# Sparse attention with a feed-forward block: keys fetched by DMA into place, values as whole rows by indexed DMA, transposes of P in two PSUM tiles

## The chip, the cores and the metric

The kernel runs on one core of one Trainium2 chip, as one launch. The metric is device time in microseconds (us). Before the change it is 954.41 us, the median of three runs (954.15 to 954.64). One further run was profiled: it took 950.94 us, and its trace spans 949.2 us from the first to the last instruction.

## The reference

Block-sparse attention feeds a layer norm and a two-layer feed-forward block (FFN) with a residual:

```python
# q, k, v: (4, 8, 768, 64) f32; sampled_blocks: (24, 3) int64, ids of key blocks of 32
scores = q @ k^T / 8
mask = |block_i - block_j| <= 1, or block_i or block_j in {0, 23},
       or block_j in sampled_blocks[block_i]
attn = softmax(where(mask, scores, -1e9)) @ v          # heads side by side: x (4, 768, 512)
xn = (x - mean) / sqrt(var + 1e-6) * g_ln
out = x + relu(xn @ w_ch1) @ w_ch2                      # w_ch1 512x2048, w_ch2 2048x512, float64
```

A query block of the middle attends eight key blocks: three sampled, block 0, its three neighbours and block 23. Query blocks 0 and 23 attend all 24. Sampled blocks are data: the program reads their ids at run time.

## The kernel before

**Tiles and visits.** Each of the 4 batches has 6 query tiles of 128 rows, in the order 1, 2, 3, 0, 4, 5. Tiles 1 to 5 (kind N) hold four middle blocks and are done in 2 visits of four heads. Tile 0 holds blocks 1, 2, 0, 23: it takes four visits of kind D (the two dense blocks, all 24 key blocks) and one of kind H (blocks 1 and 2). That is 15 visits a batch, 60 in all, counted from 0.

**A visit.** TensorE (PE) makes the scores in `ps` (L204), VectorE (DVE) the row maximum (L237, L240), ScalarE (ACT) the exponentials `p` (L247). PE transposes `p` into PSUM tile `pt` in two halves of four matmuls (L257), and ACT copies each half to SBUF (L258). One visit later PE multiplies by the values `vs` into `pv` (L267), and DVE divides by the row sum (L296 to L313). `ps` and `pt` are single PSUM tiles of two banks each.

**Keys.** All 24 key blocks of a batch lie in `kx`, loaded by plain DMA. For each N or H tile DVE copies the blocks of each query block from there into `ks` (L139 sampled, L140 neighbours, L146 blocks 0 and 23), with ids loaded into DVE registers (L122).

**Values.** Each visit of kind N or H loads its own rows of 1040 B (four heads) by DMAs that SyncE (SP) issues: one for the neighbours (L159), two or three for blocks 0 and 23 (L164), and twelve of 32 rows each whose block is a register (L179). They go into a ring of two tiles `vs`. Sampled ids that repeat a block of the mask are replaced by a block of zeros.

**FFN.** Float64 weights come as bit pairs, 1 MB pieces for w1 and 0.5 MB for w2, and are turned into an f16 high and low part by DVE (L401, L403, L405), ACT (L410, L411) and GpSimd (POOL, L412). Two w1 pieces are split in each of visits 0 to 3, four w2 pieces in each of visits 4 to 7. ACT issues the loads of all pieces but the first four. The FFN works on pairs of tiles (the first and the last tile alone): up matmuls into `pu` (L349), ACT and DVE evict (L359, L360), down matmuls into `pd` (L372).

**Order.** It is written out by a loop over steps; step s holds the scores of visit s, the value matmuls of visit s-1, and a share of the FFN's matmuls, spread over tasks such as the copies of keys, the splits and the transposes. Engines execute their instructions in that order.

Of the kernel before, what the change touches and what calls it, by code (L numbers as in the profile page):

```python
# [25 lines left out]
def sparse_attention_moe(  # L26
# [4 lines left out]
    v: bass.AP,  # L31
# [21 lines left out]
    ps_t = ctx.enter_context(tc.tile_pool(name="ps_t", bufs=1, space=bass.MemoryType.PSUM))  # L53
# [10 lines left out]
    kx = const.tile([P, NB, P], F32, name="kx")  # L64
    ks_s = ring("ks", 2, [P, 4, 8, P], F32)
# [24 lines left out]
    samp = const.tile([1, 2 * NB * NR], I32, name="samp")  # L90
    bid = const.tile([1, NB, 1], F32, name="bid")
    si = const.tile([1, NB, NR], I32, name="si")
    ei = const.tile([1, NB, NR], I32, name="ei")
    sf = const.tile([1, NB, NR], F32, name="sf")
    cf = const.tile([1, NB, NR], F32, name="cf")
    tf = const.tile([1, NB, NR], F32, name="tf")

    def index_a():
        nc.vector.tensor_copy(si, samp.rearrange("o (n r t) -> o n r t", r=NR, t=2)[:, :, :, 0])

    def index_b():
        nc.vector.tensor_copy(sf, si)
        nc.vector.tensor_tensor(out=cf, in0=sf, in1=bid.to_broadcast([1, NB, NR]),
# [14 lines left out]
        nc.vector.tensor_copy(ei, tf)  # L118

    def ids(table, eng, first, count, top):  # L120
        flat = table.rearrange("o n r -> o (n r)")[0:1, first * NR : (first + count) * NR]
        _, vals = nc.values_load_multi_w_load_instructions(  # L122
            flat, engines=[eng], min_val=0, max_val=top, skip_runtime_bounds_check_because=WHY)
        return vals

    def load_k(b, lo, hi, dma):
        dma.dma_start(kx[:, lo:hi, :], kT[b, :, lo:hi, :])

    def load_q(n, dma):
# [12 lines left out]
    def edges(t):  # L142
        ks = ks_s[t.n % 2]
        n = 2 if t.t == 0 else 4
        for s, e in ((3, 0), (7, NB - 1)):
            nc.vector.tensor_copy(ks[:, 0:n, s, :], kx[:, e : e + 1, :].to_broadcast([P, n, P]))  # L146

    def values(vi, dma):
        src, vs = v[vi.b], vi.vs
        if vi.kind == "D":  # L150
            if vi.fresh:
                dma.dma_start(vs[:, 0:6, :],
                              src[vi.hf, 0 : 6 * P, :].rearrange("(c p) e -> p c e", p=P))
            yield
            return
        if vi.kind == "N":
            i0 = vi.first
            s = src[vi.hf]
            dma.dma_start(vs[0:96, 1::2, :],  # L159
                          bass.AP(s.tensor, s.offset + (i0 - 1) * BLK * HV,  # L160
                                  [[HV, 96], [BLK * HV, 4], [1, HV]]))

            def spread(dst, blk, n):
                dma.dma_start(dst, bass.AP(s.tensor, s.offset + blk * BLK * HV,  # L164
                                           [[HV, BLK], [0, n], [1, HV]]))

            spread(vs[96:128, 0::2, :], 0, 4)
            if i0 + 3 < NB - 2:
                spread(vs[96:128, 1::2, :], NB - 1, 4)
            else:  # L170
                spread(vs[96:128, 1:7:2, :], NB - 1, 3)
                spread(vs[96:128, 7:8, :], NB, 1)
            for gg in range(4):
                if gg == 2:
                    yield
                if gg % 2 == 0:
                    reg = ids(ei, ET.SP, i0 + gg, 2, NB)
# [3 lines left out]
        else:  # L181
            sr = src.rearrange("f r e -> r f e")
            reg = ids(ei, ET.SP, 1, 2, NB)
            for gg in range(2):
                i = 1 + gg
                dma.dma_start(vs[0:96, 4 * gg + 2 : 4 * gg + 4, :],
                              sr[(i - 1) * BLK : (i + 2) * BLK])
                dma.dma_start(vs[96:128, 4 * gg + 2 : 4 * gg + 4, :],
                              sr[(NB - 1) * BLK : NB * BLK])
                e = NB if i == 1 else 0  # L190
                dma.dma_start(vs[96:128, 4 * gg : 4 * gg + 2, :], sr[e * BLK : (e + 1) * BLK])
                for r in range(NR):
                    dma.dma_start(vs[32 * r : 32 * r + 32, 4 * gg : 4 * gg + 2, :],
                                  sr[bass.ds(reg[3 * gg + r] * BLK, BLK)])
                if gg == 0:
                    yield
        yield

    def scores(vi):
        ps = vi.ps = ps_s.tile([P, 1024], F32, tag="ps", name=f"ps{vi.i}")  # L200
        q, ks = q_s[vi.tile.n % 2], ks_s[vi.tile.n % 2]
# [48 lines left out]
    def turn(vi):  # L250
        pt = ps_t.tile([P, 8, P], F32, tag="pt", name=f"pt{vi.i}")
        c = vi.shape[0] * vi.shape[1] // P
        dst = pt_s[vi.i % 2]
        for lo in range(0, c, 4):
            hi = min(c, lo + 4)
            for k in range(lo, hi):
                nc.tensor.transpose(pt[:, k, :], p_s[:, k * P : (k + 1) * P], id_sb)  # L257
            nc.scalar.copy(dst[:, lo:hi, :], pt[:, lo:hi, :])  # L258

    def attn_v(vi):  # L260
        pt, vs = pt_s[vi.i % 2], vi.vs
# [10 lines left out]
        if vi.kind == "N":  # L272
            for h in vi.heads:
                for c in range(2):
                    for gg in range(4):
                        mm(gg, h % 4, (2 * (h % 2) + h % 4 // 2) * 2 + c, 2 * gg + c, h % 4, c)
        elif vi.kind == "H":
            for pp in range(2):
                for j in range(2):
                    for c in range(2):  # L280
                        for rr in range(2):
                            h = 4 * pp + 2 * rr + j
                            for gg in range(2):
                                mm(2 * rr + gg, 2 * pp + j, (2 * j + pp) * 2 + c,
                                   4 * gg + 2 * c + h // 4, h % 4, c)
        else:
            for c in range(6):
                for rr in range(2):
                    for gg in range(2):
                        mm(2 * rr + gg, 0, c, c, 2 * rr + vi.r % 2, c)  # L290
# [44 lines left out]
    def ffn(u):  # L335
# [29 lines left out]
        for t in u.tiles:  # L365
# [3 lines left out]
            for f in range(FT):  # L369
                assert (2, f) in split  # L370
# [17 lines left out]
    con1 = stg  # L388
# [25 lines left out]
    def split_w1(i):  # L414
        fs = slice(i * 256, (i + 1) * 256)
        split_w(raw1[i % 4], con1[i % 2], w1h[:, :, fs], w1l[:, :, fs], SW1)
        split.add((1, i))
        if i + 4 < 8:
            load_w1(i + 4, nc.scalar)

    def split_w2(i):
        split_w(raw2[i % 4], con2[i % 2], w2h[:, i, :], w2l[:, i, :], SW2)
        split.add((2, i))
        if i + 4 < 16:
            load_w2(i + 4, nc.scalar)
# [14 lines left out]
    nv = 0  # L440
    for t in tiles:
        if t.t:
            plan = [("N", f, f, list(range(4 * f, 4 * f + 4))) for f in range(2)]
        else:
            plan = [("D", r // 2, r, [4 * (r // 2) + r % 2, 4 * (r // 2) + r % 2 + 2])
                    for r in range(4)] + [("H", 0, 0, list(range(8)))]
        t.visits = []
        for kind, hf, r, heads in plan:
            vi = SimpleNamespace(i=len(visits), kind=kind, hf=hf, r=r, b=t.b, tile=t,
                                 first=4 * t.t - 1, heads=heads,  # L450
                                 shape=(1, 768) if kind == "D" else (4, 256))
            vi.fresh = not (kind == "D" and r % 2)
            nv += vi.fresh
            vi.vs = vs_s[nv % 2]
            visits.append(vi)
            t.visits.append(vi)
# [8 lines left out]
    nc.sync.dma_start(samp, sampled.bitcast(I32))  # L465
    nc.scalar.dma_start(bid.rearrange("o n x -> o (n x)"), blocks)
    for lo in range(0, NB, 6):
        load_k(0, lo, lo + 6, (nc.sync, nc.scalar)[lo // 6 % 2])
    load_q(0, nc.sync)
    for i in range(4):  # L470
        load_w1(i, nc.gpsimd)
    nc.scalar.dma_start(id_sb, eye)
    nc.scalar.dma_start(g_sb, g.to_broadcast([P, DM]))
    nc.vector.memset(eps, 1e-6)
    index_a()
    index_b()
    for gg in range(4):
        keys(tiles[0], gg)
    edges(tiles[0])
    for i in range(8):  # L480
        at(i // 2, split_w1, i)
    for i in range(4):
        at(3, load_w2, i, nc.scalar)
    for i in range(16):
        at(4 + i // 4, split_w2, i)
    for t in tiles[1:]:
        prev = tiles[t.n - 1].visits
# [127 lines left out]
```

## Time and profile before

| | before |
|---|---|
| median of three runs | 954.41 us |
| profiled execution, and its span | 950.94 us, 949.2 us |
| PE busy | 737.7 us (78%) |
| DVE, ACT, POOL busy | 387.8, 283.4, 83.8 us |
| mean granted TensorE clock | 0.923 |
| DMA | 97.06 MB, mean 102 GB/s |

PE is the busiest engine. The page's slices show two regimes: in the first fifth PE is busy 1 to 5 tenths, then mostly 9, with dips to 6 to 8 that come back at even distances, once a batch.

### The profile page before, as it was taken

The page shows a single profiled execution, that of the slowest core. Times are in us where ns is not written, and L with a number is a line of the kernel's source. Part 1 is how long each engine was busy: PE and PEld are TensorE (multiplying, and loading weights), DVE is VectorE, ACT ScalarE, POOL GpSimd, SP SyncE. Part 2 cuts the span into 40 slices and gives each one's busy share as a digit, 9 for nine tenths or more (in the row PEclk, how much of TensorE's full clock was granted, in tenths as well). Part 3 has the DMA queues.
Part 4 walks back from the last instruction along what each step waited for, and adds up shares of the span by engine and source line. Part 5 has one row for each costly group of instructions (what it writes and reads, how often), then busy time and mean ns, then how long its engine had stood idle before and what let it go on. Part 6 is the DMA issues. An engine that isn't in the chain of part 4 may idle for free.

```text
span 949.2 us, 23159 instructions
## 1 busy us (share of the span) xinstructions
PE 737.7 (78%) x9344; PEld 486.4 (51%) x9344; DVE 387.8 (41%) x996; ACT 283.4 (30%) x553; POOL 83.8 (9%) x80
## 2 busy tenths in 40 slices
PE   1222455797789999996699899997699999977997
PEld 0111342473375574663375664753574755733855
DVE  5486477433434343342344252352352443342301
ACT  1243344242233232242133241332232422422201
POOL 1242223100000000000000000000000000000000
PEclk9955678899989999998799999997899999989999
DMA  8634744223643533224835432334634442234010
GB/s 302 184 117 121 215 135 133 70 59 84 158 114 61 131 78 102 57 64 101 182 73 101 108 98 73 75 66 137 129 79 110 114 113 57 58 87 95 2 32 15
DMA packets 98607, 97.06 MB, mean 102 GB/s; under 512 B 38083, under 2 KB 89412, under 8 KB 97476
## 3 DMA queue, kind: packets, MB, share of 16 engines
q1 hardware_dynamic: 92546, 71.39, 32.8%
q10 hardware_dynamic: 3458, 13.70, 4.3%
q0 software_dynamic: 2496, 10.49, 3.1%
q8 instruction: 74, 1.21, 0.6%
q14 instruction: 33, 0.27, 0.1%
HBM read 82.94 MB, written 6.29 MB: 94 GB/s over the span
## 4 chain that ended last, share of the span: by engine, by line
issue 67%; PE 8%; SPq 7%; DMA 5%; DVE 5%; POOL 4%; ACT 3%; DVEq 0%; ACTq 0%; POOLq 0%
DMA vs<-v 5%; PE pu L349 4%; SPq L179 3%; POOL xl L328 2%; SPq L122 2%; PE pt L257 1%; PE ps L204 1%; POOL out L380 1%; PE pd L372 1%; SPq L164 1%; DVE st L237 1%; ACT pt L258 1%; PE pv L267 1%; DVE ot L403 1%; ACT ot L410 1%
## 5 line engine op out<-in xcount | busy, mean ns | idle before, releaser
L257 PE MATMUL pt<-id_sb,p 128*128 128x128 f32 x448 | 78.2, 295 | 137.1 <-ACT pt L258 129.8
L349 PEld LDWEIGHTS <-w1h 128*128 128x128 f16 x1664 | 154.5, 100 | 19.3 <-issue 0.7
L247 ACT ACTIVATE p<-ps,st 128x256 f32<-128x256 f32 (+1 forms) x192 | 83.3, 510 | 262.9 <-DVE rs L296 167.8
L372 PE MATMUL pd<-w2h,hh 128*128 128x512 f16 x384 | 148.9, 388 | 0.0
L372 PE MATMUL pd<-w2h,hl 128*128 128x512 f16 x384 | 148.3, 386 | 0.0
L372 PE MATMUL pd<-w2l,hh 128*128 128x512 f16 x384 | 148.0, 385 | 0.0
L360 DVE SCALAR_TENSOR_TENSOR hl<-pu,hh 128x512 f16<-128x512 f32 x96 | 66.4, 691 | 195.1 <-ACT hh L359 195.0
L257 PEld LDWEIGHTS pt<-id_sb,p 128*128 128x128 f32 x448 | 51.8, 146 | 161.8 <-ACT pt L258 144.4
L349 PE MATMUL pu<-xth,w1h 128*128 128x256 f16 (+1 forms) x832 | 123.0, 270 | 0.0
L349 PE MATMUL pu<-xth,w1l 128*128 128x256 f16 (+1 forms) x832 | 122.5, 269 | 0.0
L372 PEld LDWEIGHTS <-hh 128*128 128x128 f16 x768 | 75.9, 99 | 89.1 <-issue 6.9
L349 PE MATMUL pu<-xtl,w1h 128*128 128x256 f16 (+1 forms) x832 | 120.9, 267 | 0.0
L267 PE MATMUL pv<-vs,pt 128*32 128x65 f32 x3584 | 79.0, 235 | 44.0 <-DMA vs<-v 43.9
L258 ACT COPY pt<-pt 128x512 f32<-128x512 f32 x120 | 67.0, 559 | 147.1 <-PE pt L257 136.1
L237 DVE TENSOR_REDUCE st<-ps 128x4 f32<-128x1024 f32 (+1 forms) x60 | 69.1, 1151 | 89.5 <-PE ps L204 89.1
L267 PEld LDWEIGHTS pv<-vs,pt 128*32 128x32 f32 x3584 | 64.3, 118 | 75.4 <-issue 59.8
L359 ACT ACTIVATE hh<-pu 128x512 f16<-128x512 f32 x96 | 57.5, 599 | 146.6 <-PE pu L349 146.6
L349 PEld LDWEIGHTS <-w1l 128*128 128x128 f16 x832 | 79.0, 100 | 9.0
L139 DVE COPY ks<-kx 128x128 f32 x264 | 56.3, 269 | 63.0 <-issue 42.5
L204 PE MATMUL ps<-ks,q 64*32 64x256 f32 x1408 | 53.3, 416 | 25.0 <-DVE ks L146 15.5
L378 DVE SCALAR_TENSOR_TENSOR ot<-pd,x 128x512 f32<-128x512 f32 x24 | 16.6, 691 | 133.8 <-PE pd L372 133.8
L328 POOL TENSOR_TENSOR xl<-xn,xh 128x512 f16<-128x512 f32 x24 | 27.6, 1151 | 458.8 <-ACT xh L327 452.8
(62 smaller groups left out, 432.2 us busy)
## 6 DMA issues: line engine op xcount, KB each, us to landing
vs<-v SPq DMA_DIRECT2D x488, 32.5 KB, 1.8
vs<-v SPq DMA_DIRECT2D x40, 390.0 KB, 4.3
vs<-v SPq DMA_DIRECT2D x72, 130.0 KB, 4.3
vs<-v SPq DMA_DIRECT2D x8, 780.0 KB, 4.6
q<-qT SPq DMA_DIRECT2D x24, 256.0 KB, 2.9
out<-ot POOLq DMA_DIRECT2D x24, 256.0 KB, 2.4
kx<-kT SPq DMA_DIRECT2D x6, 768.0 KB, 7.5
stg<-w ACTq DMA_DIRECT2D x8, 512.0 KB, 3.8
```

The source lines that it names most:

```text
L139: cp(ks[:, gg, r : r + 1, :], kx[:, bass.ds(t.reg[3 * (gg % 2) + r], 1), :])
L204: nc.tensor.matmul(ps[32 * part : 32 * part + 32, col : col + n], lhs[64 * row : 64 * row + 64], rhs[64 * row : 64 * row + 64], start=True ...
L237: nc.vector.tensor_reduce(out=st[:, 0:n], in_=vi.ps[:, 0 : n * w].rearrange("p (h k) -> p h k", k=w), axis=AX.X, op=ALU.max, negate=True)
L247: nc.scalar.activation(p_s[:, hs], vi.ps[:, hs], AF.Exp, bias=vi.st[:, 4 + h : 5 + h], scale=0.125)
L257: nc.tensor.transpose(pt[:, k, :], p_s[:, k * P : (k + 1) * P], id_sb)
L258: nc.scalar.copy(dst[:, lo:hi, :], pt[:, lo:hi, :])
L267: nc.tensor.matmul(pv[32 * row : 32 * row + 32, 65 * col : 65 * col + 65], pt[:, ch, 32 * row : 32 * row + 32], vs[:, vv, 65 * e : 65 * e ...
L328: nc.gpsimd.tensor_sub(xl, xn, xh)
L349: nc.tensor.matmul(ph[:, j * n : (j + 1) * n], w[:, ct, fs], x[:, ct, 0:n], start=m == 0, stop=m == 3 * CT - 1, skip_group_check=True)
L359: nc.scalar.activation(dh, ph, AF.Relu)
L360: nc.vector.scalar_tensor_tensor(out=dl, in0=ph, scalar=0.0, in1=dh, op0=ALU.max, op1=ALU.subtract)
L372: nc.tensor.matmul(po, x[:, f, ts], w[:, f, :], start=m == 0, stop=m == 3 * FT - 1)
```

## The change

- **Keys.** `kx` and the DVE copies are gone. `ks` is a ring of two tiles of 32 blocks. For an N or H tile SP issues one DMA for the neighbours (1536 B pieces) and 12 (H: 6) of one block each, 128 partitions of 512 B, with register ids. Blocks 0 and 23 stand in a small tile `kg` per batch and POOL copies them in (L168). For the dense blocks the 24 blocks are loaded into a ring tile in two DMAs.
- **Values.** One load per job (a tile; tile 0 is two jobs, H then D) instead of one per visit, with rows of 2080 B (eight heads). The sampled and block-0 rows of one query block come by one indexed DMA that POOL issues, 128 rows each, four per N tile (L192). DVE works out the row numbers once at the start.
- **When.** The loads of the next job are issued in the step of the first visit of the present one.
- **Transposes.** `pt` is one bank, in a pool of two; each half takes a tile of its own. As long as no FFN work is queued, they stand ahead of the splits in their step.
- **Weights.** POOL issues all weight loads; w1's splits use four buffers instead of two.

```diff
@@ keys and values
-        for r in range(NR):
-            cp(ks[:, gg, r : r + 1, :], kx[:, bass.ds(t.reg[3 * (gg % 2) + r], 1), :])
-        cp(ks[:, gg, 4:7, :], kx[:, i - 1 : i + 2, :])
+        for gg in range(n):
+            for r in range(NR):
+                nc.sync.dma_start(kv[:, gg, r, :], src[:, bass.ds(reg[NR * gg + r], 1), :]
+                                  .rearrange("p o e -> p (o e)"))
             yield
...
-                    dma.dma_start(vs[32 * r : 32 * r + 32, 2 * gg, :],
-                                  s[bass.ds(reg[3 * (gg % 2) + r] * BLK, BLK), :])
+        for gg, i in enumerate(job.blocks):
+            nc.gpsimd.indirect_dma_start(
+                out=vs[:, 2 * gg, :], out_offset=None, in_=src,
+                in_offset=bass.IndirectOffsetOnAxis(ap=rows[:, i : i + 1], axis=0))
@@ turn
-        pt = ps_t.tile([P, 8, P], F32, tag="pt", name=f"pt{vi.i}")
...
+            pt = ps_t.tile([P, 4, P], F32, tag="pt", name=f"pt{vi.i}_{lo}")
@@ weights
-    con1 = stg
+    con1 = [stg[0], stg[1], late[0], late[1]]
...
-            load_w1(i + 4, nc.scalar)
+            load_w1(i + 4, nc.gpsimd)
@@ the step
-            k = len(tasks) // 2
-            tasks = tasks[:k] + [(turn, (vi,))] + tasks[k:]
+            nxt = jobs[vi.job.i + 1] if vi is vi.job.visits[0] and vi.job.i + 1 < len(jobs) else None
+            pre = []
+            if nxt:
+                gen = keys(nxt)
+                pre = [(next, (gen, 0)), (values, (nxt,))] + [(next, (gen, 0))] * 6
+            tasks = pre + tasks
+            if queue:
+                k = len(tasks) // 2
+                tasks = tasks[:k] + [(turn, (vi,))] + tasks[k:]
+            else:
+                tasks = [(turn, (vi,))] + tasks
```

Three places in the programs. The first is SP's queue at one N load. Before, a visit's value rows (names: out<-in, `vs_82` is one tile of the ring; an ISA row works out an address, and twelve such pairs follow each other with one more register load):

```order
L130 DMA q_88<-qT 128x512
L159 DMA vs_82<-v 96x4x260
L164 DMA vs_82<-v 32x4x260 x2
L122 TENSOR_LOAD ei
L179 ISA
L179 DMA vs_82<-v 32x260
```

Now, the load of a whole tile, where twelve pairs for keys follow, then the next queries and the transposes of the norm's output:

```order
L144 DMA ks_79<-kT 128x4x384
L180 DMA vs_83<-v 96x4x520
L188 DMA vs_83<-v 32x4x520
L149 TENSOR_LOAD si
L153 ISA
L153 DMA ks_79<-kT 128x128
...
L171 DMA q_88<-qT 128x512
L331 DMA_TRANSPOSE xth<-xh_96 128x4x128
L332 DMA_TRANSPOSE xtl<-xl_98 128x4x128
```

So SP issues twelve register DMAs a tile instead of 24, and they carry keys; the sampled values have left this queue.

The second is ACT in the first step. Before, from the exponentials of visit 0 (`p<-ps`) to the copies of its transposes:

```order
L247 ACTIVATE p<-ps_195,st_212 128x256 x4
L410 ACTIVATE stg_105<-stg_105 128x1024
L411 CAST w1h<-stg_105 128x4x256
L393 DMA w2h<-w 128x2048
L410 ACTIVATE stg_106<-stg_106 128x1024
L411 CAST w1h<-stg_106 128x4x256
L393 DMA w2h<-w 128x2048
L258 COPY pt_85<-pt_274 128x512 x2
```

Now:

```order
L246 ACTIVATE p<-ps_202,st_219 128x256 x4
L257 COPY pt_86<-pt_0_226 128x512
L257 COPY pt_86<-pt_4_232 128x512
L411 ACTIVATE stg_106<-stg_106 128x1024
L412 CAST w1h<-stg_106 128x4x256
L411 ACTIVATE stg_107<-stg_107 128x1024
L412 CAST w1h<-stg_107 128x4x256
```

The two copies have moved ahead of the step's splits, and the weight loads have left ACT.

The third is PE at the transposes of a visit in mid FFN. Before, the six of visit 6 go to one PSUM tile:

```order
L349 LDWEIGHTS w1h
L349 MATMUL pu_12_1233<-xtl,w1h 128x128
L257 MATMUL pt_1342<-id_sb,p 128x128 x6
L349 LDWEIGHTS w1h
L349 MATMUL pu_12_1233<-xth,w1h 128x128
```

Now, the eight of visit 6 (which is the H visit here) go to two tiles:

```order
L373 LDWEIGHTS hh
L373 MATMUL pd_1124<-w2h,hh 128x512
L256 MATMUL pt_0_1126<-id_sb,p 128x128 x4
L256 MATMUL pt_4_1132<-id_sb,p 128x128 x4
L373 LDWEIGHTS hl
L373 MATMUL pd_1124<-w2h,hl 128x512
```

The second half names a tile of its own, `pt_4`, so nothing of the first half's copy stands between the two.

## Rows read from the trace of the kernel before

**Rows 1.** Busy time by stretch: engines, granted clock, DMA share, GB/s

```profile
177.00:949.20 772.20, 675.46 (x8389) 446.81 (x8388) 278.22 (x775) 218.79 (x446) 37.40 (x45) 0.96 0.38 88
0.00:177.00 177.00, 62.24 (x959) 39.62 (x959) 109.56 (x221) 64.63 (x107) 46.43 (x35) 0.77 0.54 163
```

**Rows 2.** Waits of PE from 177 us on: us, times, longest

```profile
PE pv L267 <- DMA vs<-v: 43.9, 29, 3.2
PE pt L257 <- ACT pt L258: 37.7, 52, 1.3
PE ps L204 <- issue: 9.5, 3, 3.6
```

**Rows 3.** Timeline of a steady visit: start, us, instructions, [idle before <- releaser]

```profile
411.17 1.09 PE L204 MATMUL ps<-ks,q 64*32 64x256 f32 x32
...
415.44 0.60 PE L257 MATMUL pt<-id_sb,p 128*128 128x128 f32 x4
...
416.71 0.66 PE L257 MATMUL pt<-id_sb,p 128*128 128x128 f32 x4 [0.68 <-ACT pt L258]
...
421.08 1.09 PE L204 MATMUL ps<-ks,q 64*32 64x256 f32 x32
```

**Rows 4.** Timeline of SP's queue and PE behind the D and H visits

```profile
432.37 7.78 SPq L179 DMA_DIRECT2D vs<-v  x12
...
435.78 0.27 PE L267 MATMUL pv<-vs,pt 128*32 128x65 f32 x2 [3.16 <-DMA vs<-v]
```

**Rows 5.** Waits of PE from 0 to 177 us

```profile
PE pt L257 <- ACT pt L258: 92.1, 8, 17.7
```

**Rows 6.** Timeline of PE: scores of visits 4, 5 and 8 and one wait

```profile
93.21 1.12 PE L257 MATMUL pt<-id_sb,p 128*128 128x128 f32 x4 [16.50 <-ACT pt L258]
94.26 1.96 PE L204 MATMUL ps<-ks,q 64*32 64x256 f32 x32
...
117.78 1.09 PE L204 MATMUL ps<-ks,q 64*32 64x256 f32 x32
...
176.98 1.28 PE L204 MATMUL ps<-kx,q 64*32 64x512 f32 x12
```

**Rows 7.** Timeline of DVE and POOL in steps 0, 1 and 6

```profile
24.38 2.85 POOL L412 TENSOR_TENSOR w1l<-stg,w1h 128x1024 f16<-128x1024 f32 x1 [20.84 <-ACT w1h L411]
...
25.63 1.96 DVE L139 COPY ks<-kx 128x128 f32 x3 [0.37 <-issue]
...
27.77 0.49 DVE L139 COPY ks<-kx 128x128 f32 x3
...
41.55 1.23 DVE L237 TENSOR_REDUCE st<-ps 128x4 f32<-128x1024 f32 x1 [13.02 <-PE ps L204]
...
43.63 0.68 DVE L401 TENSOR_SCALAR stg<-w2l 128x1024 int32<-128x1024 int32 x1
...
45.60 1.23 DVE L405 SCALAR_TENSOR_TENSOR stg<-w2l,stg 128x1024 int32<-128x1024 int32 x1
...
141.46 0.42 DVE L401 TENSOR_SCALAR ot<-hh 128x512 int32<-128x512 int32 x1
...
150.04 0.69 DVE L405 SCALAR_TENSOR_TENSOR ot<-stg,ot 128x512 int32<-128x512 int32 x1
```

**Rows 8.** DMA queue 1 in 403:416 and 453:457 us: packets, MB, share of 16 engines

```profile
q1 hardware_dynamic: 1307, 1.15, 38.9%
...
q1 hardware_dynamic: 337, 1.23, 95.8%
```

**Rows 9.** DMA issues: count, KB each, median us to landing

```profile
vs<-v SPq DMA_DIRECT2D x488, 32.5 KB, 1.8
...
out<-ot POOLq DMA_DIRECT2D x24, 256.0 KB, 2.4
```

**Rows 10.** Groups of POOL: busy us, mean ns | idle before

```profile
L328 POOL TENSOR_TENSOR xl<-xn,xh 128x512 f16<-128x512 f32 x24 | 27.6, 1151 | 458.8 <-ACT xh L327 452.8 <-issue 6.0
...
L380 POOL DMA_DIRECT2D out<-ot x24 | 13.3, 553 | 290.0 <-DVE ot L378 290.0
```

More of the change, by code (lines that the diff above doesn't have):

```diff
@@ new lines, in index_b, with keys @@
+        nc.vector.tensor_copy(rows, rf)
+    def keys(job):
+        ks, b = job.ks, job.b
+        if job.kind == "D":
+            for lo in (0, 12):
+                nc.sync.dma_start(ks[:, lo * P : (lo + 12) * P].rearrange("p (n e) -> p n e", e=P),
+                                  kT[b, :, lo : lo + 12, :])
+                yield
+            return
+        kv = ks.rearrange("p (g s e) -> p g s e", s=8, e=P)
+        n = len(job.blocks)
+        i0 = job.blocks[0]
+        src = kT[b]
+        if job.kind == "N":
+            edges(job, kv)
+        nc.sync.dma_start(kv[:, 0:n, 4:7, :],
+                          bass.AP(src.tensor, src.offset + (i0 - 1) * P,
+                                  [[NB * P, P], [P, n], [1, 3 * P]]))
+        yield
+        flat = si.rearrange("p n r -> p (n r)")[0:1, i0 * NR : (i0 + n) * NR]
+        _, reg = nc.values_load_multi_w_load_instructions(
+            flat, engines=[ET.SP], min_val=0, max_val=NB - 1, skip_runtime_bounds_check_because=WHY)
+        for gg in range(n):
+            for r in range(NR):
+                nc.sync.dma_start(kv[:, gg, r, :], src[:, bass.ds(reg[NR * gg + r], 1), :]
+                                  .rearrange("p o e -> p (o e)"))
+            yield
+        if job.kind == "H":
+            edges(job, kv)
+        yield
@@ L339, in ffn @@
         step = 512 // n
-        c1 = 109 if n == 256 else 100
+        c1 = 109 if n == 256 else 84
         for f in range(0, FT, step):
-            assert all((1, x // 2) in split for x in range(f, f + step))
+            while any((1, x // 2) not in split for x in range(f, f + step)):
+                yield -1
             ph = ps_f.tile([P, 512], F32, tag="pf", name=f"pu{u.i}_{f}")
@@ L439, in sparse_attention_moe, with add @@
         n += k
-    nv = 0
+    jobs = []
+    def add(t, kind, blocks, plan):
+        k = len(jobs)
+        job = SimpleNamespace(i=k, kind=kind, b=t.b, blocks=blocks, ks=ks_s[k % 2], vs=vs_s[k % 2],
+                              visits=[])
+        jobs.append(job)
+        for hf, r, heads in plan:
+            vi = SimpleNamespace(i=len(visits), kind=kind, hf=hf, r=r, b=t.b, tile=t, job=job,
+                                 heads=heads, shape=(1, 768) if kind == "D" else (4, 256))
+            visits.append(vi)
+            job.visits.append(vi)
+            t.visits.append(vi)
     for t in tiles:
+        t.visits = []
         if t.t:
-            plan = [("N", f, f, list(range(4 * f, 4 * f + 4))) for f in range(2)]
-        else:
[L445 to L456, printed above, removed]
+            add(t, "N", list(range(4 * t.t - 1, 4 * t.t + 3)),
+                [(f, f, list(range(4 * f, 4 * f + 4))) for f in range(2)])
+        else:
+            add(t, "H", [1, 2], [(0, 0, list(range(8)))])
+            add(t, "D", [0, NB - 1], [(r // 2, r, [4 * (r // 2) + r % 2, 4 * (r // 2) + r % 2 + 2])
+                                      for r in range(4)])
     NV = len(visits)
@@ L463, in at @@
         todo.setdefault(step, []).append((fn, args))
[L465 to L469, printed above, removed]
+    nc.sync.dma_start(samp, sampled.bitcast(I32).to_broadcast([P, 2 * NB * NR]))
+    load_kg(0)
+    load_q(0)
+    nc.scalar.dma_start(bid, blocks)
+    nc.scalar.dma_start(id_sb, eye)
+    nc.scalar.dma_start(g_sb, g.to_broadcast([P, DM]))
     for i in range(4):
         load_w1(i, nc.gpsimd)
-    nc.scalar.dma_start(id_sb, eye)
-    nc.scalar.dma_start(g_sb, g.to_broadcast([P, DM]))
     nc.vector.memset(eps, 1e-6)
+    nc.vector.memset(rf, 0.0)
     index_a()
+    for _ in keys(jobs[0]):
+        pass
     index_b()
-    for gg in range(4):
-        keys(tiles[0], gg)
-    edges(tiles[0])
+    values(jobs[0])
     for i in range(8):
@@ L486, in sparse_attention_moe @@
     for t in tiles[1:]:
-        prev = tiles[t.n - 1].visits
-        s = prev[0].i
-        at(s, load_q, t.n, nc.sync)
-        first = t.n % 6 == 0
-        if first:
-            for lo in (0, 12):
-                at(s, load_k, t.b, lo, lo + 12, nc.sync)
-        n = 2 if t.t == 0 else 4
-        for gg in range(n):
-            at(prev[min(len(prev) - 1, (n + gg if first else 2 * gg) // n)].i, keys, t, gg)
-        if t.t in (1, 2, 5, 0):
-            at(prev[-1].i, edges, t)
+        at(tiles[t.n - 1].visits[0].i, load_q, t.n)
+    for b in range(1, B):
+        at(tiles[6 * b - 2].visits[0].i, load_kg, b)
     queue, nextu, s = [], 0, 0
@@ L537, in sparse_attention_moe @@
         if vi:
-            for _ in values(vi, nc.sync):
-                pass
             softmax(vi)
```

173 lines of the change are left out of this document (76 added, 97 removed).

## The prediction

> **What bounds the kernel now.** I read the page's slices first, then busy time by stretch, PE's waits, and timelines of one visit in each regime. I cut the span at 176.98 us, where the scores of visit 8 begin [rows 6]: by then the weight splits are done. Before the cut PE is busy 62 of 177 us at a mean clock of 0.77; behind it 675.5 of 772.2 us at 0.96 [rows 1]. So there are two problems.
>
> Behind the cut PE is the bound and only loses time to waits: 43.9 us for values, 37.7 us in 52 transposes, 9.5 us in scores that stand behind key copies [rows 2], together 91.1 us. Idle time is 772.2 - 675.5 = 96.7 us, so 5.6 us are left for the end. The transposes' wait is in every visit: first half at 415.44, second at 416.71 after 0.68 us for ACT's copy of the first half [rows 3]. The waits for values come in the visits that follow tile 0: SP takes 7.78 us to issue twelve register DMAs, and PE starts its value matmuls in pieces, as they land [rows 4].
>
> Before the cut nothing is busy all the time; a chain is. PE waits 92.1 us in eight visits for the copy of the first half [rows 5], 16.50 us in one of them [rows 6]: ACT has that copy behind the step's splits, those wait for DVE, and DVE also copies keys.
>
> **The change part by part.** The sum is made against the profiled execution's span of 949.2 us. That run took 950.94 us, 1.7 more, and the median shown is 954.41, another 3.5 more; both are added at the end.
>
> *Transposes in two tiles, behind the cut.* The second half names another PSUM tile, so the wait goes: 52 visits, 37.7 us. What is next for PE is FFN work, which needs neither. Between 0 and 37.7 us; I take all of it.
>
> *Values and keys a job ahead, behind the cut.* The waits of 43.9 and 9.5 us go, since loads are issued in the step of the present job's first visit. What is late next: the DMA itself. From two windows [rows 8]: 1307 packets took 0.389 x 13 us x 16 engines = 81 us, 62 ns each at a mean of 880 B; 337 packets took 61 us, 182 ns each at 3650 B. A line through both is 24 ns + 0.043 ns per byte. So an N tile now costs 1536 packets of 512 B x 46 ns = 71, 512 of 1536 B x 90 = 46, 1024 of 2080 B x 114 = 117, queries and output 256 x 113 = 29: 263 engine-us, over 16 engines 16.4 us. Before it was 2048 x 69 + 29 = 170, or 10.6 us.
>
> A visit behind tile 0 is 421.08 - 411.17 = 9.9 us long [rows 3], 9.2 without the transposes' wait, so a tile of two visits gives 18.4 us. The load needs some 2 us until the last job's value matmuls free the tile, 16.4 us, and about 2 us to land [rows 9]: 20.4. That is 2 us late, and the norm's transposes stand behind the keys in SP's queue; I put 3 us on each of eight such tiles (two a batch), 24 us. Elsewhere (the four visits of D, or pairs with more FFN work to a visit) there is more time. Bounds: 0, and 53.4 (as much as now).
>
> SP's own part shrinks: one such group of twelve register DMAs a tile (7.78 us and about 4 for the rest) instead of two. The waiting instruction added to SP is the neighbours' value load, for the value matmuls of the job before; keys, queries and transposes queue behind it, and PE waits for those.
>
> The Trainium skill ("DMA: Bandwidth & Descriptors", Rules for kernel authors) says that transfers under 64 KB are mostly overhead; key DMAs are 64 KB each. Were twelve of them paid one after the other at the 2 us that this page fits as fixed cost, a tile would take 24 us and be 6 us late in each of the eight, 24 us more than I take. The trace disagrees for SP's queue: twelve of 32.5 KB are issued in 7.78 us and each lands 1.8 us after its issue, so they overlap.
>
> *Clock behind the cut.* Granted 0.96 of full speed over 772.2 us [rows 1] is 31 us of full-speed work. The dips come behind idle stretches, and PE is at full speed in the steady ones. I take three quarters, 23 us; between 0 and 31.
>
> Behind the cut: 675.5 + 5.6 - 23 + 24 = 682 us.
>
> *Before the cut, visits 0 to 3.* A step of DVE is the maximum 1.23, four small ones of the two visits (41.55 to 43.63 less the 1.23: 0.9) and two w1 splits from 43.63 to 46.83, 3.2 each [rows 7]: 8.6 us. The key copies, 1.96 us for three in the bad case [rows 7], are gone. ACT copies the transposes before the splits, and w1 has four buffers. If the first scores stand at 20 us (an estimate; the first keys now come as 512 B pieces beside 4 MB of weights), four steps end at 54 us. But the DMA must carry three N tiles (49 us) and 8.4 MB of w1; by the window with large packets (1.23 MB in 3.83 us, 321 GB/s) that is 26 us. Together 75 us: DMA decides. Scores of visit 4 at 76 us instead of 94.26 [rows 6]. Bounds 54 and 94.
>
> *Visits 4 to 7.* The first took 117.78 - 94.26 = 23.5 us, much of it for the first w2 pieces, which are still loaded only at the end of step 3; less some 3.5 us of key copies, 20. In the other three DVE needs the maximum and small ones 2.1, four w2 splits 9.3 (141.46 to 150.73) [rows 7], norm and eviction 1.5: 13 us, 39 together. So the cut moves to 76 + 20 + 39 = 135 us, 42 earlier. Bounds: 113 (DMA free) and 177.
>
> POOL gets four gathers an N tile. The nearest row is its own DMA of 128 rows of 2 KB, 0.553 us [rows 10]; four are 2.2 us, with two copies of the size of L328 (1.15 each) and xl about 6 us a tile. POOL is idle enough: 37.4 us of 772.2 busy [rows 1]. DVE's 98 us of key copies behind and before the cut do nothing for the time by themselves.
>
> The DVE copy took 1.96 us for three while POOL's subtraction ran from 24.38 to 27.23, and 0.49 at 27.77 [rows 7]: one holds up the other. The Trainium skill ("SBUF — State Buffer", Who interferes with whom) says that such DVE copies and a GpSimd operation lock each other out for a whole instruction; the trace agrees. By that rule POOL's gathers could be held by a DVE operation each time, but the change takes away most of DVE's copies, so the rule speaks for it here; the sum is unchanged.
>
> Sum: 135 + 682 = 817 us of span, 819 profiled, **822 us** as a median.
>
> **Rivals.** *DMA takes SP's place.* PE waits for keys and values as long as now, 53.4 us, and the clock falls as now: 135 + 675.5 + 5.6 + 53.4 = 870, as a median 875. For it: 35 MB more in 512 and 1536 B pieces, D's 3.2 MB prefetched in the one visit of H. Against: behind the cut the DMA is busy 0.38 [rows 1]. Chance 0.17.
>
> *The start stays.* POOL now has splits, weight loads, key copies and gathers in one order, and a gather waits for PE's value matmuls; a weight load behind it is late. The cut stays at 177: 177 + 682 = 859, median 864. Against: the 92.1 us were ACT's order [rows 5], which is changed. Chance 0.12.
>
> *The transposes still wait*, for the exponentials or for ACT: 37.7 us more, 860. The two tiles are apart in the order of PE, so 0.04.
>
> *Gathers are dear on POOL: slower.* At X us each a tile costs POOL 4X + 4 us. PE gives a tile of two visits 682 / 52 x 2 = 26 us, so POOL decides from X = 5.5. It is slower than before when 26 such pairs exceed 949 - 135 = 814 us, 31 us each, X = 6.8, twelve times the 0.553 of rows 10. At 7.5 us: 26 x 34 + 135 + 5 = 1024 us. Nothing in the trace shows a gather, so 0.05.
>
> **How the numbers follow.** Forecast 0.62, rivals 0.17, 0.12, 0.04 and 0.05. The forecast's own range is 784 to 860: its low end has the start at 118, new waits of 10 us and the whole 31 us of clock (118 + 660 + 5), its high end a start at 150 and the clock unchanged (150 + 705 + 5). The range of 784 to 878 takes in the first three rivals. A difference under 0.2% can't be told from none. Faster 0.94 (all but the last), within 0.2% 0.01, slower 0.05.
>
> **What would show it.** PE's waits: transposes for ACT near 0 behind visit 8, values near 0, and what is left stands at scores or at the FFN's first up matmuls of the pair behind tile 0. Scores of visit 4 near 76 and of visit 8 near 135 us, the DMA near full up to the former. Granted clock behind visit 8 above 0.98. POOL's gather near 0.6 us; 3 us or more is a warning. It is wrong if scores wait for keys by 5 us or more in most tiles, if visit 8 stays near 170, or if POOL's queue ends the waits of PE.

## The result and the profile after

The changed kernel takes 817.98 us (817.17 to 826.0), the kernel before 954.28 in the same group of runs: a ratio of 0.860, interval 0.854 to 0.865. The forecast was 822. Run once more with later experiments it took 811.9 us (810.42 to 817.51) against 951.01, a ratio of 0.855 (0.851 to 0.859). So a difference of some 6 us between kernels of different groups of runs says nothing here; where one matters below, ratios to the kernel before, run beside each, are compared.

The profiled execution of 817.5 us has a span of 815.7. Busy time by stretch, cut where the scores of visit 8 begin (columns as in [rows 1]):

```profile
0.00:145.34 145.34, 69.03 (x991) 44.08 (x991) 93.21 (x151) 65.42 (x110) 82.19 (x83) 0.77 0.87 269
145.34:815.70 670.36, 648.88 (x8355) 439.75 (x8354) 221.01 (x467) 212.90 (x443) 128.62 (x153) 0.99 0.52 139
```

Against [rows 1] the start is 31.7 us shorter and the rest 101.8 us. Both rests hold the same FFN work (1105 down and 2304 up matmuls); the small difference in PE's count is from tile 0, which now begins with its H visit. Behind the cut PE is idle for 21.5 us, not 96.7, and the granted clock is 0.99. What PE still waits for there (us, times, longest; it answers to [rows 2]):

```profile
PE ps L203 <- DMA q<-qT: 4.4, 3, 2.0
PE pd L373 <- issue: 3.6, 4, 1.0
PE ps L203 <- issue: 3.4, 3, 1.9
PE pv L266 <- issue: 1.7, 3, 0.7
PE ps L203 <- DMA ks<-kT: 1.7, 2, 1.2
PE ps L203 <- DVE ot L379: 1.3, 1, 1.3
```

Neither values nor the copies of the transposes are left in it. The list sums to 16.1 us, nearly all in the two tiles behind each tile 0 (the thin tiles below, of two short visits). In a steady visit the eight transposes now stand in one piece, where [rows 3] has two with 0.68 us between them:

```profile
269.17 1.09 PE L203 MATMUL ps<-ks,q 64*32 64x256 f32 x32
...
275.62 1.04 PE L256 MATMUL pt<-id_sb,p 128*128 128x128 f32 x8
...
282.70 1.09 PE L203 MATMUL ps<-ks,q 64*32 64x256 f32 x32
```

The start by visits, PE's timeline (visits 0, 2 and 4, then 7 and 8; it answers to [rows 6]):

```profile
22.72 1.07 PE L203 MATMUL ps<-ks,q 64*32 64x256 f32 x4 [22.72 <-DMA ks<-kT]
...
50.01 2.30 PE L203 MATMUL ps<-ks,q 64*32 64x256 f32 x32 [8.06 <-DMA q<-qT]
...
72.72 2.29 PE L203 MATMUL ps<-ks,q 64*32 64x256 f32 x32 [4.18 <-DMA q<-qT]
...
119.83 1.49 PE L203 MATMUL ps<-ks,q 64*32 64x512 f32 x16
...
145.34 2.79 PE L203 MATMUL ps<-ks,q 64*32 64x512 f32 x16
```

PE's waits there, up to 145.34 us, against the 92.1 of [rows 5]:

```profile
PE pt L256 <- ACT p L246: 28.4, 7, 8.8
PE ps L203 <- DMA ks<-kT: 24.5, 4, 22.7
PE ps L203 <- DMA q<-qT: 12.2, 2, 8.1
PE pd L373 <- POOL w2l L413: 4.5, 2, 4.0
```

The wait on the PSUM tile is gone and a shorter one for the exponentials has come. The first is for keys, and q is late behind them on SP. SP's timeline has why: its twelve register DMAs of job 0 and of job 1 (64 KB each) take twice as long to issue as the 7.78 us of [rows 4] (32.5 KB each). The DMA is busy 0.92 of the first 72.72 us.

```profile
8.00 15.98 SPq L153 DMA_DIRECT2D ks<-kT  x12
...
29.41 14.72 SPq L153 DMA_DIRECT2D ks<-kT  x12
44.18 0.43 SPq L171 DMA_DIRECT2D q<-qT  x1
```

POOL's new group, beside [rows 10] (busy us, mean ns | idle before it):

```profile
L192 POOL DMA_INDIRECT vs<-v,rows x88 | 87.9, 998 | 99.1 <-PE pv L266 60.5 <-issue 33.0 <-DVE rows L128 4.6
```

### The profile page after: what moved, and what is told of

Same layout as the page of the kernel before. It is cut to its first block, busy times and chain, and to the rows that moved or that the text cites. A ratio compares the mean times of both kernels' runs of the same rounds, so it can differ in the third digit from the quotient of the medians.

```text
span 815.7 us, 21773 instructions
## 1 busy us (share of the span) xinstructions
PE 717.9 (88%) x9344; PEld 483.8 (59%) x9344; DVE 314.2 (39%) x618; ACT 278.3 (34%) x553; POOL 210.8 (26%) x236
## 4 chain that ended last, share of the span: by engine, by line
PE 55%; issue 20%; DMA 13%; POOL 5%; SPq 4%; DVE 2%; ACT 1%; POOLq 0%
PE pu L349 24%; PE pd L373 16%; PE ps L203 7%; DMA vs<-v 6%; PE pv L266 5%; PE pt L256 4%; DMA ks<-kT 4%; SPq L153 3%; DMA q<-qT 2%; POOL w2l L413 2%; POOL vs L192 1%; DVE ot L404 1%; POOL xl L327 1%; DMA samp<-sampled 1%; POOL ks L168 0%
## 5 line engine op out<-in xcount | busy, mean ns | idle before, releaser
L203 PE MATMUL ps<-ks,q 64*32 64x256 f32 (+1 forms) x1664 | 83.5, 420 | 47.6 <-DMA ks<-kT 26.2
L349 PE MATMUL pu<-xth,w1l 128*128 128x256 f16 (+1 forms) x832 | 120.6, 266 | 0.0
L349 PE MATMUL pu<-xth,w1h 128*128 128x256 f16 (+1 forms) x832 | 120.6, 266 | 0.0
L192 POOL DMA_INDIRECT vs<-v,rows x88 | 87.9, 998 | 99.1 <-PE pv L266 60.5
L256 PE MATMUL pt<-id_sb,p 128*128 128x128 f32 x448 | 67.5, 293 | 28.4 <-ACT p L246 28.4
L203 PEld LDWEIGHTS ps<-ks,q 64*32 64x32 f32 x1664 | 34.8, 110 | 85.6 <-issue 75.0
L257 ACT COPY pt<-pt 128x512 f32<-128x512 f32 x120 | 62.1, 564 | 64.7 <-PE pt L256 56.9
L256 PEld LDWEIGHTS pt<-id_sb,p 128*128 128x128 f32 x448 | 54.9, 149 | 40.1 <-ACT p L246 33.4
L379 DVE SCALAR_TENSOR_TENSOR ot<-pd,x 128x512 f32<-128x512 f32 x24 | 16.6, 690 | 156.5 <-PE pd L373 156.5
L266 PEld LDWEIGHTS pv<-vs,pt 128*32 128x32 f32 x3584 | 56.5, 112 | 32.9 <-issue 24.1
L266 PE MATMUL pv<-vs,pt 128*32 128x65 f32 x3584 | 67.9, 225 | 5.1 <-issue 2.9
```

The costliest lines, as they stand in the source:

```text
L192: nc.gpsimd.indirect_dma_start(out=vs[:, 2 * gg, :], out_offset=None, in_=src, in_offset=bass.IndirectOffsetOnAxis(ap=rows[:, i : i + 1], ...
L203: nc.tensor.matmul(ps[32 * part : 32 * part + 32, col : col + n], lhs[64 * row : 64 * row + 64], rhs[64 * row : 64 * row + 64], start=True ...
L256: nc.tensor.transpose(pt[:, k - lo, :], p_s[:, k * P : (k + 1) * P], id_sb)
L257: nc.scalar.copy(dst[:, lo:hi, :], pt[:, 0 : hi - lo, :])
L266: nc.tensor.matmul(pv[32 * row : 32 * row + 32, 65 * col : 65 * col + 65], pt[:, ch, 32 * row : 32 * row + 32], vs[:, vv, 65 * e : 65 * e ...
L349: nc.tensor.matmul(ph[:, j * n : (j + 1) * n], w[:, ct, fs], x[:, ct, 0:n], start=m == 0, stop=m == 3 * CT - 1, skip_group_check=True)
```

## The experiments

**Each part alone.** One PSUM tile again, all else as changed:

```
-ps_t bufs=2;  pt = ps_t.tile([P, 4, P]) for each half
+ps_t bufs=1;  pt = ps_t.tile([P, 8, P]) for both halves
```

> The changed kernel with P's transposes in one PSUM tile of eight chunks, as before the change; keys, values and rings as changed. Theory: behind visit 8 PE again waits for the copy of the previous four chunks at every visit that has filler between its halves, 0.7 us a visit, the 37.7 us that before shows there (52 visits); nothing else takes up that time, so the time is 817.5 + 38 = 855 (850 to 862). Rival: in the changed kernel the transposes stand where ACT has long caught up, or the thin visits' value waits absorb it: under 830. Second rival: one tile also holds up the start, where PE waits for ACT behind the softmax: a further 10 to 40, so 865 to 895.

Measured 845.07 us, ratio 0.8865 (0.8845 to 0.8884). Behind visit 8 (146.6 us) the only wait that PE's list still has is the old one, its total and count as in [rows 2]:

```profile
PE pt L256 <- ACT pt L257: 37.7, 52, 1.1
```

The stretch is 696.0 us long against 670.4, so 25.6 of the 37.7 us count: the changed kernel's own 16.1 us of waits are not in it, and PE is busy 4.0 us longer (37.7 - 16.1 + 4.0 = 25.6). Against the changed kernel's second trace, whose stretch is 662.8 us, it is 33.2. That slower visits give the loads more time is the likely reason and was not tested by itself. The start does not change (visit 8 at 146.6). The theory had the mechanism and the size of the wait, but the time is below its range: its "nothing else takes up that time" is wrong. Now the kernel before with two PSUM tiles and nothing else:

> The kernel before with this part alone: P's transposes in two PSUM tiles of four chunks each. Theory: the 37.7 us of PE's waits for the transposes' copies behind the start go, the 43.9 us of waits for values stay, and the start, which its key and value loads and the splits set, keeps its 177 us: 954.3 - 38 = 916 (908 to 924). Rival A: the 92.1 us that PE waits for the same copy in the start go too, because one tile made them: 830 to 870. Rival B: the waits for values take up what the transposes give back: 940 to 955.

Measured 911.16 us, ratio 0.9562 (0.9541 to 0.9582), as the theory has it, but not in its places. Behind the cut (164.1 us) it is 745.8 us, 26.4 shorter than before and not 37.7, since other waits grow, those for values from 43.9 to 49.9; visit 8 starts 12.9 us earlier. So the parts alone bring about 108 us (everything but the PSUM tiles, from the first run) and 42; together they bring 136 to 139. The 108 were not split up further: what the order of the transposes, the four buffers of w1, the weight loads on POOL and the missing key copies each give to the start was not run.

**The lead of the loads.**

```
-nxt = jobs[i + 1] if vi is vi.job.visits[0] ...
+nxt = jobs[i + 1] if vi is vi.job.visits[-1] ...
```

> The changed kernel with the next job's key and value loads issued at the job's last visit and not at its first: the rings of two hold the same, but the loads start one visit later (three for a thin job's four visits). Theory (the second tile of each ring pays only by the lead it gives): an N tile's loads want about 16 us of the DMA engines, a visit lasts 10 to 12 us, so PE waits 3 to 6 us for keys or values in each of some 40 tiles behind the start, and visits 1 to 8 start later by about as much: 817.5 + 100 to 240, at the least 880. Rival (the direct form alone pays, its lead hardly matters): under 840.

Measured 902.91 us, ratio 0.9486 (0.946 to 0.9513). PE's waits and busy time behind visit 8 (152.1 us):

```profile
PE ps L203 <- DMA ks<-kT: 66.9, 18, 10.3
```
```profile
152.10:898.00 745.90, 671.65 (x8355) 446.28 (x8354) 221.50 (x467) 212.52 (x443) 130.75 (x159) 0.94 0.47 126
```

The stretch is 745.9 us, as long as in the run before it (745.8), which had the old loads: without the lead the new form of the loads brings nothing behind the start. The theory's direction and floor of 880 hold; its tiles that wait were too many (18 waits, not some 40 tiles), so the 100 to 240 us became 85. The same asked of the kernel before, where the form stays and the lead comes:

```
-for _ in values(vi, nc.sync): pass
+for nv in (visits[0:2] if s == 0 else visits[s + 1 : s + 2]):
+    for _ in values(nv, nc.sync): pass
```

> The kernel before with one edit: the values of visit s+1 are issued in step s, not in step s+1 itself, so a value load has a lead of two visits as in the changed kernel; its form (register DMAs of 32.5 KB on SP, halves), the keys and the transposes stay. Theory (the lead pays, the form only makes room for it): the 43.9 us of waits for values behind the start go mostly, and with them the some 23 us that the lower clock took: 885 to 905. Rival (the form pays: twelve register DMAs take SP 7.8 us and the rest 4, a visit behind tile 0 is 9.9 us long, so SP's queue stays late whatever the lead): 925 to 954.

Measured 924.77 us, ratio 0.9718 (0.9691 to 0.9744), between the two, 0.2 us under the rival's range. PE's waits behind visit 8 (from 170.5 us):

```profile
PE ps L204 <- DVE ks L146: 41.5, 3, 14.4
PE pt L257 <- ACT pt L258: 37.8, 52, 1.3
PE pv L267 <- DMA vs<-v: 5.8, 5, 1.4
```

The lead does take the waits for values (5.8 us are left of 43.9), but SP's queue is as full as before, and the next batch's keys now stand behind those values. The timeline shows it (SPq issues):

```profile
233.44 8.91 SPq L179 DMA_DIRECT2D vs<-v  x12
242.40 0.42 SPq L130 DMA_DIRECT2D q<-qT  x1
242.93 0.84 SPq L127 DMA_DIRECT2D kx<-kT  x2
...
254.71 1.92 PE L204 MATMUL ps<-ks,q 64*32 64x256 f32 x26 [14.42 <-DVE ks L146]
```

So the lead pays, and the form is what leaves SP room for it: both theories hold in part. Not tested is the old form with the lead and the next batch's keys issued ahead of the values; part of the 41.5 us may be this order and not the form.

**What makes the start.** First q ahead of the keys on SP:

```
-at(tiles[t.n - 1].visits[0].i, load_q, t.n)
+if s in qload: tasks = [(load_q, (qload[s],))] + tasks
```

> The changed kernel with the next tile's q load issued on SP ahead of that tile's key loads, not behind them. In the start SP's twelve register DMAs take 8 to 16 us to issue, q stands behind them, and PE waited 16.6 us for q (8.1 at visit 2, 4.2 at visit 4, the rest at three others). Theory: these waits are on the path, so 8 to 16 us go: 802 to 810. Rival (the DMA engines are full in the start, q's turn is another load's delay; keys, splits or weights then end the same waits): within 3 us of 817.5.

Measured 809.09 us, ratio 0.848 (0.8446 to 0.8514); beside 0.855 (0.851 to 0.859) for the unedited kernel this is inconclusive. In its trace the waits for q are gone and those for keys have grown from 26.2 to 37.8 us, and visit 8 starts at 145.6 us: the rival holds for the start. The time lies in the theory's range, but what is shorter lies behind visit 8 (662.9 us, and 662.8 when the unedited kernel ran again). Then, on top of it, the loads of step 7 behind that step's splits (q of the tile behind tile 0 as in the changed kernel):

```
-tasks = pre + tasks
+tasks = tasks + pre if s == 7 else pre + tasks
```

> The changed kernel with q ahead of the keys (as in the run with q first, 809.1 us; here not for the tile behind each tile 0, whose D keys lost 1.8 us to it), and at step 7 the next job's key and value loads issued behind the step's four weight splits, not ahead of them. Theory: at step 7 POOL does key copies and four gathers of 1.0 us between the splits' subtractions, DVE waits 4.6 us for that and PE 6.3 us: visit 8 starts at 139 to 141 us instead of 145.5, and the time is 800 to 805. Rival (the loads that stand later make the next tiles' keys late, or ACT ends the step at the same time): 806 to 812.

Measured 798.78 us, ratio 0.8385 (0.8354 to 0.8416): better than the changed kernel, and than q first alone by 1%. The reason can be read from POOL in step 7. In the changed kernel two key copies and four gathers part the subtractions, and PE waits:

```profile
126.04 1.17 POOL L413 TENSOR_TENSOR w2l<-ot,w2h 128x512 f16<-128x512 f32 x1
...
130.87 1.27 POOL L192 DMA_INDIRECT vs<-v,rows  x1 [0.16 <-issue]
...
136.42 2.27 POOL L413 TENSOR_TENSOR w2l<-ot,w2h 128x512 f16<-128x512 f32 x2
137.63 0.58 PE L373 MATMUL pd<-w2l,hh 128*128 128x512 f16 x1 [4.01 <-POOL w2l L413]
```

In the edited one the splits run through, gathers follow, and visit 8 starts at 140.23 us:

```profile
131.11 1.41 POOL L413 TENSOR_TENSOR w2l<-ot,w2h 128x512 f16<-128x512 f32 x1 [3.13 <-ACT w2h L412]
...
132.57 0.38 PE L373 MATMUL pd<-w2l,hh 128*128 128x512 f16 x1 [0.90 <-POOL w2l L413]
...
140.23 2.36 PE L203 MATMUL ps<-ks,q 64*32 64x512 f32 x12
140.92 1.01 POOL L192 DMA_INDIRECT vs<-v,rows  x1 [0.15 <-issue]
```

Of the 10.6 us of span against q first, 5.4 are in the start, as expected, 3.5 of them in step 7 (25.0 us there, 21.5 here); the other 5.2 lie behind visit 8, in the range in which groups of runs differ.

Next, fewer bytes:

```
-if i + 4 < 8:  load_w1(i + 4)      -if i + 4 < 16: load_w2(i + 4)
+if i + 4 < 4:  load_w1(i + 4)      +if i + 4 < 4:  load_w2(i + 4)
```

> The changed kernel without the loads of w1's pieces 4 to 7 and w2's pieces 4 to 15 (their splits run on the pieces that lie in the buffers): 10 of 16.8 MB of weights are not read. Theory, as the prediction has it (DMA decides until visit 4): 4 MB of w1 less is 13 us at 321 GB/s, so the scores of visit 4 start near 60 us, not 72.7; steps 4 to 7 keep their 72 us, since splits, gathers and exponentials make them, and the time is near 805. Rival (the splits' chain over DVE, ACT and POOL makes the first four steps too): visit 4 within 3 us of 72.7, the time 814 to 820.

Measured 807.15 us, ratio 0.8479 (0.845 to 0.8507). The time is near the theory's 805, the place is not: visit 4 starts at 69.44 us, visit 8 at 145.1, though the DMA's share from 75 to 145 us falls from 0.83 to 0.56. Behind visit 8 it is 8.5 us shorter with the same program; hence the unedited kernel again:

> The changed kernel once more, unedited, beside the runs of this group. If its time is a property of the kernel: 816 to 820, visit 8 at 145 us and some 16 us of waits behind it. The run without most of the weights was 8.5 us faster behind visit 8, where its program is the same; if that comes from the chip or the hour and not from the kernel, this run is nearer to 808.

Measured 811.9 us: visit 8 at 148.4, 662.8 us behind it, against 661.9 of the run with few weights. So those 8.5 us were not of the edit, and visit 8 moves by 0 to 3 us for 10 MB less. Of the two, the rival is nearer in the start. Last, two edits on top of the best: the first four w1 splits ahead of visit 0, later ones two steps earlier; and w1's pieces 2 and 3 loaded behind job 0's gathers.

> The run with the step's splits first (798.8 us), with the first four w1 splits ahead of visit 0 and each later split two steps earlier; in the steps that have w2 splits the next job's loads stand behind them. DVE sits idle for 18.6 us before the maximum of visit 0, since that waits for the first keys; a w1 split takes it 3.2 us. Theory (the chain of the splits through DVE, ACT and POOL sets the start, from the first maximum to visit 8): four splits, 12.9 us, are done in that idle time, and visit 8 starts near 127 us instead of 140.2: 784 to 790. Rival (the DMA decides: the pieces come no earlier, as first keys and first values stand beside them): visit 8 at 136 or later, 794 or more.

Measured 798.5 us, ratio 0.8392 (0.8365 to 0.842): no gain, in the rival's range. Visit 8 starts at 145.67 us, 5.4 later, and the stretch behind it is 5.4 us shorter. The splits did run in DVE's idle time (from 11.04 us on), but that calls for w1's pieces 4 to 7 sooner, and visit 2 waits for its keys:

```profile
53.29 2.50 PE L203 MATMUL ps<-ks,q 64*32 64x256 f32 x12 [5.58 <-DMA ks<-kT]
```

> The run with the step's splits first (798.8 us), with the loads of w1's pieces 2 and 3 issued on POOL behind job 0's gathers, not at the program's start: 2 of the 4 MB that stand ahead of the first keys in the DMA engines. Theory: by 321 GB/s the first keys come 6 us earlier, the scores of visit 0 start at 16 to 18 us, not 22.6, and the start from there on moves along: visit 8 at 134 to 137 us, the time 793 to 796. Rival (the DMA engines carry the same bytes until visit 4, in whatever order): first scores earlier, but visit 4 within 2 us of 68 and visit 8 within 2 us of 140; 797 to 801. Worse still if pieces 2 and 3 now come too late for the splits of step 1: visit 2 later than 42 us, over 801.

Measured 818.86 us, ratio 0.8587 (0.8546 to 0.8628), the worst of the cases expected (visit 2 late, over 801). The first scores come 8 us earlier, and job 1's keys pay for it, beside weights that are later as well:

```profile
14.69 1.69 PE L203 MATMUL ps<-ks,q 64*32 64x256 f32 x8 [14.69 <-DMA ks<-kT]
...
53.00 1.06 PE L203 MATMUL ps<-ks,q 64*32 64x256 f32 x4 [14.41 <-DMA ks<-kT]
```

So until visit 2, some 42 to 56 us in these kernels, the loads decide (the DMA is 0.97 busy up to visit 2 in the changed kernel), and what was moved up in these two runs was paid by the next in the queue. Bytes alone do not tell it: in the run with fixed keys below, visit 2 starts at 42.34 us with the same bytes in all and the same share of 0.97. There, though, visit 8 starts at 144.64 us: what is gained at visit 2 does not reach it. From visit 2 to visit 8 it is the engines' chain in the changed kernel: 10 MB less leave it as long as it was, and moving step 7's loads shortens it. What set the same stretch in the run with the early splits (92 us, though 13 us of DVE's splits lay ahead of it) stays open.

**The forms of the sampled loads.** One fixed DMA of three blocks a group in place of the register DMAs:

```
-for r in range(NR): nc.sync.dma_start(kv[:, gg, r, :], src[:, bass.ds(reg[...], 1), :])
+nc.sync.dma_start(kv[:, 0:n, 0:3, :], <three neighbouring blocks a group>)
```

> The changed kernel with the sampled key blocks of N and H jobs loaded by one fixed DMA of three neighbouring blocks each (the chosen ids are not followed; the bytes are the same) in place of the twelve register DMAs. Theory: the register DMAs cost only by the queries behind them on SP, so this gives what q first gave: 806 to 812. Rival A: their 512 B pieces load the DMA engines as well; 1536 B pieces take 46 instead of 71 engine-us a tile, 1.6 us less on each of the eight thin tiles and 5 in the start: 792 to 803. Rival B: nothing of SP's issue is on the path: 815 to 820.

Measured 801.7 us, ratio 0.8431 (0.8406 to 0.8457): rival A. Behind visit 8 (144.6 us) 2.7 us of waits for keys and none for q are left, and the stretch is 653.7 us, 9 to 17 shorter than in the two runs of the changed kernel. So the register DMAs cost it 10 to 16 us; issue and packet size were not told apart. The same for values, in place of POOL's gathers:

```
-nc.gpsimd.indirect_dma_start(out=vs[:, 2 * gg, :], in_=src, in_offset=rows[:, i])
+nc.sync.dma_start(vs[:, 0 : 2 * n : 2, :], <128 fixed rows a group>)
```

> The changed kernel with the sampled value rows loaded by one fixed DMA on SP a job (the chosen ids are not followed; the bytes are the same, rows of 2080 B), so POOL has no gathers. Theory: a gather's 1.0 us on POOL decides only at step 7, where four stand between the splits: visit 8 starts near 140 us instead of 145.3, behind it nothing changes (POOL is 19% busy there): 810 to 814. Rival A: POOL's gathers are hidden in step 7 too: 816 to 820. Rival B: SP's value DMA now waits for the last value matmuls and holds keys, queries and transposes behind it as the neighbours' does: no more than that, but if the DMA engines take fixed rows faster than gathered ones, the 16 us of new waits behind visit 8 go as well: 798 to 805.

Measured 824.83 us, ratio 0.866 (0.8607 to 0.8713): above all three ranges, and not clearly different from the gathers' 0.860 (0.854 to 0.865). PE's waits in the whole run:

```profile
PE ps L202 <- DMA q<-qT: 35.3, 6, 17.9
```

Another 520 to 1040 KB stand on SP ahead of the keys and q of each job (the twelve register DMAs of job 1 take 19.64 us to issue, not 14.72). Waits for q are 35.3 us, not 16.6, the longest 17.9 at visit 2. That takes up what POOL gains, and it does gain in step 7: from visit 7 to visit 8 it is 21.7 us here, where it is 25.5 with gathers. DVE's waits in that step, with gathers and without:

```profile
DVE ot L402 <- POOL w2l L413: 5.6, 2, 4.6
```
```profile
DVE ot L401 <- POOL w2l L412: 2.1, 2, 1.0
```

The key copies stand where they stood, so it is the gathers that hold the splits in step 7. On the whole they are worth their microsecond on POOL, since they go round SP; that they are the faster form, the times do not show.

## Why the prediction was right, and where it was not

*Transposes, 37.7 us.* Right: the first run gives exactly this wait back. It is not additive, though: of the 37.7, 25.6 or 33.2 come back in time, by which of the changed kernel's two traces is taken; the rest is taken up by its waits for loads.

*Waits for keys and values, -53.4 + 24.* The mechanism was right, the new term mis-sized: 16.1 us, and 9.1 when run again (3.1 for q, 2.0 DVE, 1.9 keys, 1.2 and 0.9 others), nearly all in the thin tiles, as forecast; q and keys are the largest part, and none is at the FFN's first up matmuls. The Trainium skill ("DMA: Bandwidth & Descriptors", Rules for kernel authors) calls transfers under 64 KB mostly overhead. As the prediction weighed it, paid one after the other, it would have made these tiles wait twice as long as forecast; the runs disagree with that.

*Clock, -23.* PE is busy 648.9 us behind the cut instead of 675.5, so 26.6. That is near the forecast in part by luck, since not all of it is the clock. Transposes and values, before and after (count, busy us, mean ns, idle before):

```profile
L257 PE MATMUL pt<-id_sb,p 128*128 128x128 f32 x388 | 63.6, 282 | 37.8 <-ACT pt L258 37.7
L267 PE MATMUL pv<-vs,pt 128*32 128x65 f32 x3152 | 71.0, 236 | 44.0 <-DMA vs<-v 43.9
```
```profile
L256 PE MATMUL pt<-id_sb,p 128*128 128x128 f32 x386 | 53.2, 275 | 0.0
L266 PE MATMUL pv<-vs,pt 128*32 128x65 f32 x3136 | 57.4, 223 | 1.7 <-issue 1.7
```

The transposes take 10.4 us less, and with one PSUM tile again they take 62.3 at a granted clock of 1.00: some 9 us are the two halves that became one piece, a gain that the prediction had at nothing. That leaves some 17 us for the clock and all else.

Behind the cut, then, 648.9 + 16.1 + 5.4 for the rest = 670.4, where the forecast had 682: 3.6 from PE's busy time, 8 from the waits.

*DMA decides until visit 4, 76 us.* The time is right (72.7 us, 74.2 when run again), the reason at most up to visit 2: without 10 MB of weights visit 4 comes 3 us earlier, not 13.

*Visits 4 to 7: 20 + 3 x 13.* This is the step that failed. The four took 9.5, 19.2, 18.4 and 25.5 us, 72.6 in all, 14 more than forecast. The first was short, as the first w2 pieces were there. For the other three the step counted DVE's work alone (13 us each). By stretch:

```profile
82.24:101.39 19.15, 10.36 (x186) 8.98 (x184) 15.39 (x26) 9.95 (x19) 11.06 (x14) 0.73 0.77 284
101.39:119.83 18.44, 11.60 (x158) 7.02 (x157) 12.63 (x22) 10.61 (x20) 7.26 (x9) 0.81 0.88 266
119.83:145.34 25.51, 14.75 (x117) 6.04 (x117) 17.20 (x29) 11.01 (x20) 17.99 (x18) 0.65 0.86 231
```

DVE's busy time, the third column of these, is 45.2 of 63.1 us, where the step had 39 in all. DVE's waits between visits 4 and 8 name what was left out:

```profile
DVE hl L360 <- ACT hh L359: 8.0, 4, 2.8
DVE ot L402 <- POOL w2l L413: 7.7, 4, 4.6
```

The FFN starts in these steps, and its evictions stand in DVE's queue behind ACT; and a split needs one of two buffers that POOL frees, with step 7's gathers between. The latter is shown twice: step 7 takes 21.5 us with the loads behind the splits and 21.7 without gathers, not 25.5. That is 4 of the 24 us that these three steps took beyond their 39; the former was only read from the trace, and what makes the rest stays open. So the sum of 817 us for a span of 815.7 is in part luck: 10 us too short in the start, 12 too long behind it.

*The gather, 0.6 us.* It takes 1.0. Behind the start POOL is busy 128.6 of 670 us, and none of PE's waits there is ended by it; in the start it ends 4.5 us of them, 4.0 of it in step 7.

Rivals: the start did not stay and the transposes do not wait. PE's waits for loads, which *DMA takes SP's place* had, come when the lead is taken away (66.9 us for keys, granted clock 0.94).

## What to carry to other kernels

When loads are late, ask first how long before their use they are issued, and then whether the queue that issues them has room for that lead: here the form without the lead brought 8 us, the lead in the old form 26, and both some 93. In a start where several in-order engines pass work around, adding up the busiest engine's work is too little; go through each queue for what stands between its links, and put loads behind them if what they bring is not wanted soon (two w1 pieces put behind job 0's gathers made the best kernel 20 us slower). A wait that goes is partly spent on a wait that it had been hiding, so part gains do not add up (42 + 108 us became 136 to 139).

## What was not expected of the hardware

Not all waits lower the clock. With 52 waits of up to 1.1 us (37.7 us in all) the granted clock behind visit 8 is 1.00; with 49.9 us in 33 waits of up to 3.6 us, which lie close together in the visits behind tile 0, and 14.1 us in five others, it is 0.95. The busy time of the two rows differs by 23.7 us, though the first has 8 us more in its transposes (the loads differ between the two as well). In the kernel before the granted clock is 0.50 from 438 to 442 us, which is 1.2 of 2.4 GHz, with waits of 3.16 and 1.13 us for values ahead of it and of 2.54 us into it; 58 value matmuls then take 1.91 us, and 1.07 at 453.64 us, at 1.00. The rows, one PSUM tile first, then two with the old loads:

```profile
146.60:842.60 696.00, 652.90 (x8355) 435.46 (x8354) 220.99 (x467) 217.99 (x443) 128.63 (x153) 1.00 0.50 134
```
```profile
164.10:909.90 745.80, 676.62 (x8389) 452.74 (x8388) 278.67 (x776) 213.74 (x446) 37.41 (x45) 0.95 0.38 91
```

The same DMAs take a queue more or less time to issue: twelve 64 KB register DMAs take SP 15.98 us from 8.00 us on, and 7.72 us behind tile 0, from 202.72 us on (1.33 and 0.64 us each). How full the DMA is does not tell them apart: its share is 1.04 in the first and 1.05 in the second (392 and 309 GB/s). What does was not tested.
